# Attention and squared-ReLU MLP on one core: the first chunk's softmax on other engines, and another order of weights and third-chunk work on GpSimd

## The chip, the core and the metric

The kernel runs on one core of a Trainium2 chip. The metric is the device time of one execution in microseconds (us), the median of three runs. The engines are TensorE (PE in the profile: matrix products; PEld: its weight loads), VectorE (DVE), ScalarE (ACT), GpSimd (POOL) and SyncE (SP, which issues the DMAs). SBUF is the on-chip memory, PSUM the banks in which TensorE writes its products.

## The reference

```python
# q, k, v: (8 batches, 8 heads, 576 positions, 64), fp32
scores = q @ k.T / 8
mask_local   = (rel >= 0) & (rel < 32)                    # heads 0 to 3, rel = i - j
mask_strided = (rel >= 0) & (j % 32 == i % 32)            # heads 4 to 7
attn = exp(masked scores - max);  attn /= attn.sum() + 1e-9
x = (attn @ v), heads side by side        # 4608 tokens x 512
h = maximum(x @ w_in, 0)                  # w_in 512 x 2048
out = h * h @ w_out                       # w_out 2048 x 512
```

## The kernel before

The 4608 tokens are cut into 12 chunks of 384. A chunk's attention output x is kept transposed, in a local and a strided half (`xl`, `xs`), each as a high and a low fp32r part (`xlh`, `xll`, `xsh`, `xsl`: the low part is the value less its high part). The MLP of a chunk runs over 16 slices j of 128 hidden units: `up(c, j)` makes 12 products of 128x384 (L462: high by high, low by high, high by low, for four slices of the model dimension), then the squared ReLU and the split into `gh` and `gl` (L470 to L476), and `down(c, j)` adds 9 products of 128x512 to three PSUM accumulators (L489). These 192 steps set TensorE's work.

The weights arrive as raw 64-bit integers and are turned into high and low fp32r parts on the chip during the first chunk, by the generator `convert()`: per half tile a scaling on ScalarE (L154, per whole tile), a conversion into a PSUM bank on ScalarE (`z`, L166), a merge on VectorE that reads that bank (L169), the high cast on ScalarE (L172) and the low subtraction on GpSimd (L173). The weights come in the order w_in 0, w_in 1, w_out 0, w_in 2, w_out 1, and so on; in the rows `w_0`, `w_1` and so on stand for w_in's tiles as for w_out's, numbered apart.

The first chunk's attention has four generators of `pe_pair`, each for two heads: `first` (two local pairs, b_0_1 and b_1_1) and `late` (two strided pairs, b_0_0 and b_1_0). One step of each makes loads, scores and minima (L319, L324), one the exponentials and the normalisation (L345 to L353), one the transposes T and their copies `pt` (L359, L360), one the output products and the split into high and low (L367 and L378, L382 and L383). Local pairs use one exponential per window with its sum taken along (`single`, L345), strided pairs subtract the minimum on GpSimd (L347) and take one exponential per head (L348). The code ahead of the loop calls these steps in an order written out by hand, with runs of zero products (`zeros`, L586) in between, which keep TensorE occupied.

The second chunk has two local pairs of the same kind, and all further chunks `pe_head`. The strided half of later chunks is made by `strided(c)` with elementwise work: products on GpSimd (`pq`, L412), sums on VectorE (L413), a small softmax (L418 to L425), products again (`pp`, L434), sums, transposes, a cast and a subtraction on GpSimd (L446) that writes `xsl`. The blocks 2 and 3 (`pq_2`, `pq_3`) are in the first chunk's time the strided half of the second chunk. `take(c + 2, "010")` starts the heads of the third chunk: their first GpSimd instructions are the subtractions of `kx` and `qx` (L218, L220), which the score products `s` (L234) read.

Each engine runs its instructions in one order. A scheduler sets it when the kernel is built, from the order of the code, the data's dependencies and the marks `issue_after` (an instruction issued no earlier than another); `behind` puts such a mark around one step of a generator. `psum(i, ...)` gives bank i of five. `up` takes the banks 0, 1 and 2 in turn, which hold the first chunk's scores and outputs at the start.

## Time and profile before

| | |
|---|---|
| median of three runs | 884.83 us (883.32 to 884.88) |
| profiled execution | 883.18 us, its span 881.4 us |
| TensorE busy | 868.5 us, 99% of the span |
| VectorE, ScalarE, GpSimd busy | 635.5, 572.6, 676.8 us |

The span goes from the first to the last instruction of the profiled execution; the execution's own time has 1.78 us around it. The shares are averages over a head without dense products (to 30 us), the first chunk with the weights' conversion (to about 114 us), ten chunks that look alike, and the end.

### The profile page before, as it was taken

What the parts mean: (1) busy time and instruction counts of PE and PEld (TensorE: products, weight loads), DVE (VectorE), ACT (ScalarE), POOL (GpSimd) and SP (SyncE); (2) the same over time, 40 slices, a digit from 0 to 9 for tenths busy, and PEclk for the clock granted to TensorE, in tenths of its full rate; (3) what the DMA queues carried; (4) which work ended last, traced back from release to release, by engine and by line L of the source; (5) the groups of instructions that cost most, each with busy time, mean ns of one, the idle gap of its engine ahead of it and who ended that gap; (6) DMA issues with size and microseconds to landing.
All of it is one profiled execution on the core that took longest, in us unless ns stands there. A gap on an engine that the chain in (4) does not pass through costs nothing.

```text
span 881.4 us, 14862 instructions
## 1 busy us (share of the span) xinstructions
PE 868.5 (99%) x4744; PEld 789.6 (90%) x4744; DVE 635.5 (72%) x1892; ACT 572.6 (65%) x1510; POOL 676.8 (77%) x722
## 2 busy tenths in 40 slices
PE   8899999999999999999999999999999999999997
PEld 7788899999999999999999999999999989998996
DVE  4578687788777888878778778778787787883111
ACT  6798776676676666757657747657666665664332
POOL 4698878878978989898988978997898899782000
PEclk9999999999999999999999999999999999999999
DMA  9851631323123123104102302312131121000000
GB/s 356 355 195 63 184 121 42 103 84 113 32 66 112 37 89 103 44 30 127 44 13 80 115 14 74 104 31 74 31 102 57 30 71 61 7 1 10 28 1 36
DMA packets 26798, 71.41 MB, mean 81 GB/s; under 512 B 2976, under 2 KB 8736, under 8 KB 25184
## 3 DMA queue, kind: packets, MB, share of 16 engines
q1 hardware_dynamic: 26432, 70.14, 23.9%
q8 instruction: 37, 0.61, 0.3%
q10 hardware_dynamic: 288, 0.33, 0.1%
q14 instruction: 41, 0.34, 0.1%
HBM read 61.01 MB, written 9.44 MB: 80 GB/s over the span
## 4 chain that ended last, share of the span: by engine, by line
PE 95%; ACT 3%; DVE 1%; POOL 0%; issue 0%; DVEq 0%; POOLq 0%; ACTq 0%
PE h L462 44%; PE y L489 44%; PE s L234 2%; PE o L280 2%; ACT e L345 1%; PE w_ps L586 1%; ACT raw L154 1%; PE b L319 1%; DVE sc L419 0%; ACT z L166 0%; ACT w L172 0%; DVE raw L169 0%; ACT pt L360 0%; PE b L359 0%; DVE xsl L383 0%
## 5 line engine op out<-in xcount | busy, mean ns | idle before, releaser
L489 PE MATMUL y<-w,gh 128*128 128x512 f32 x1152 | 357.1, 391 | 0.8 <-ACT gh L475 0.8
L489 PEld LDWEIGHTS y<-w,gh 128*128 128x128 f32 x1152 | 212.5, 188 | 41.5 <-ACT gh L475 1.4
L462 PE MATMUL h<-xlh,w 128*128 128x384 f32 x768 | 229.6, 339 | 2.1 <-DVE xsl L383 1.6
L462 PE MATMUL h<-xsh,w 128*128 128x384 f32 x768 | 226.2, 335 | 0.0
L489 PE MATMUL y<-w,gl 128*128 128x512 f32 x576 | 224.0, 392 | 0.0
L434 POOL TENSOR_TENSOR pp<-vs,sc 128x448 f32<-128x448 f32 (+10 forms) x192 | 189.8, 1014 | 39.8 <-DVE qs L435 18.2
L412 POOL TENSOR_TENSOR pq<-ks,qs 128x512 f32<-128x512 f32 (+2 forms) x192 | 197.8, 1050 | 17.9 <-DVE sc L413 13.8
L476 DVE TENSOR_TENSOR gl<-h,gh 128x384 fp32r<-128x384 f32 x192 | 105.4, 550 | 84.2 <-ACT gh L475 82.9
L475 ACT CAST gh<-h 128x384 fp32r<-128x384 f32 x192 | 91.4, 477 | 103.0 <-PE y L489 100.0
L473 ACT ACTIVATE h<-h 128x384 f32<-128x384 f32 x176 | 83.0, 472 | 107.8 <-PE h L462 106.2
L413 DVE TENSOR_REDUCE sc<-pq 128x8 f32<-128x512 f32 (+4 forms) x228 | 119.6, 534 | 46.2 <-POOL pq L412 43.9
L462 PEld LDWEIGHTS h<-xlh,w 128*128 128x128 f32 x768 | 142.1, 188 | 5.6 <-DVE xsl L383 1.8
L462 PEld LDWEIGHTS h<-xsh,w 128*128 128x128 f32 x768 | 141.7, 188 | 0.3
L462 PE MATMUL h<-xll,w 128*128 128x384 f32 x384 | 129.3, 337 | 0.0
L435 DVE TENSOR_REDUCE qs<-pp 128x64 f32<-128x448 f32 (+11 forms) x192 | 106.7, 563 | 31.0 <-POOL pp L434 29.5
L489 PEld LDWEIGHTS y<-w,gl 128*128 128x128 f32 x576 | 108.1, 188 | 22.9
L462 PE MATMUL h<-xsl,w 128*128 128x384 f32 x384 | 128.5, 335 | 0.0
L474 ACT ACTIVATE h<-h 128x384 f32<-128x384 f32 x176 | 83.2, 473 | 3.6
L259 DVE STREAM_TRANSPOSE p_t<-e 32x128 f32<-32x128 f32 x240 | 72.3, 301 | 10.4 <-ACT e L248 6.0
L462 PEld LDWEIGHTS h<-xll,w 128*128 128x128 f32 x384 | 72.5, 189 | 2.2
L462 PEld LDWEIGHTS h<-xsl,w 128*128 128x128 f32 x384 | 72.2, 188 | 0.0
L243 ACT ACTIVATE e<-e,nm 96x128 f32<-96x128 f32 x160 | 62.5, 392 | 10.5 <-DVE nm L226 8.8
(97 smaller groups left out, 1077.2 us busy)
## 6 DMA issues: line engine op xcount, KB each, us to landing
qk<-qk_l SPq DMA_DIRECT2D x24, 400.0 KB, 3.2
y<-ysb SPq DMA_DIRECT2D x36, 256.0 KB, 3.7
raw<-w_in SPq DMA_DIRECT2D x7, 1024.0 KB, 11.2
qk<-qk_l SPq DMA_DIRECT2D x16, 416.0 KB, 3.3
vs<-v_s SPq DMA_DIRECT2D x10, 576.0 KB, 4.0
raw<-w_out SPq DMA_DIRECT2D x5, 1024.0 KB, 12.9
v<-v_l SPq DMA_DIRECT2D x40, 128.0 KB, 2.0
ks<-k_s SPq DMA_DIRECT2D x8, 576.0 KB, 3.8
```

Of the source, the lines that this page charges most:

```text
L243: nc.scalar.activation(e[:QC, cut(w)], e[:QC, cut(w)], AF.Exp, bias=nmax[:QC, w : w + 1], scale=-1.0, accum_out=ssum[:QC, w, :1])
L259: nc.vector.transpose(out=pt[STR * k : STR * (k + 1), :, STR * r : STR * (r + 1)], in_=e.rearrange("p (w k) -> p w k", k=KW)[STR * r : STR ...
L412: nc.gpsimd.tensor_mul(pv, kt[:, a : a + m, :], qt[:, i - i0 : i - i0 + 1, :].broadcast_to([P, m, D]))
L413: nc.vector.tensor_reduce(out=sc[:, i - i0, a : a + m], in_=pv, op=ALU.add, axis=AX.X)
L434: nc.gpsimd.tensor_mul(pv, vt[:, a : a + nd, :n], sc[:, il : il + 1, :n].broadcast_to([P, nd, n]))
L435: nc.vector.tensor_reduce(out=ot[:, il, a : a + nd], in_=pv, op=ALU.add, axis=AX.X)
L462: done = nc.tensor.matmul(ph[:, :TC], w[:, wsl], xx, start=n == 0, stop=n == 11)
L473: nc.scalar.activation(g, g, AF.Relu)
L474: nc.scalar.activation(g, g, AF.Square)
L475: last["gh"] = nc.scalar.copy(gh, g)
L476: nc.vector.tensor_sub(gl, g, f32(gh))
L489: done = nc.tensor.matmul(y_ps[c][t], g[:, sl], w[:, wsl], start=j == 0 and k == 0, stop=j == NFT - 1 and k == 2)
```

## The change

In the first chunk the local pairs' exponentials go to PSUM, into the pair's score banks, and VectorE, no longer GpSimd, multiplies them from there by the reciprocal sums into SBUF. The copies of the transposed probabilities of both strided pairs and of local pair 0 (six of eight) move from ScalarE to VectorE. Two runs of 30 zero products become one run of 60 in bank 1 behind the first strided pair's scores. The order of the head's steps is another: the second local pair's exponentials stand behind the first pair's, the second strided pair's scores behind the first pair's multiplies. The split of the first weight is called at once. `up` takes the banks two places on. The weights of a step are no longer asked for behind the strided work of the same step alone: they are gated by `gh` up to step 13 (and by the strided subtraction `xs` in step 13), the heads of the third chunk are started behind them, and the two clears of `p_t` stand behind the last weight on GpSimd. Lines below L177 of before stand 3 to 10 lines further down in the new code (L351 is the old L345, L360 the old L353, L366 and L367 the old L359 and L360, L374 the old L367, L385 the old L378, L419 the old L412, L441 the old L434, L453 the old L446, L469 the old L462); the text names old lines where it doesn't say otherwise.

```diff
--- before.py
+++ after.py
@@ -174,6 +174,9 @@
                     if at and 4 <= k < 12:
                         fetch(k + 4)
 
+                if k == 0 and at:
+                    split()
+                    split = None
                 if not at and k + 1 < NFT and k + 1 in raws:
                     with tc.issue_after(first_step.ins):
                         scale(k + 1)
@@ -313,7 +316,10 @@
         ss = sums[sm]
 
         s_ps = [banks() for _ in range(2)] if c == 0 else None
-        e4 = [e[:QC, : NW * kw].rearrange("p (w k) -> p w k", k=kw) for e in es]
+        blocks = lambda t: t[:QC, : NW * kw].rearrange("p (w k) -> p w k", k=kw)
+        e4 = [blocks(e) for e in es]
+
+        r4 = [blocks(t) for t in s_ps] if single else e4
         def scores(h, w, s):
             rows = slice(D * h, D * (h + 1))
             last["p"] = nc.tensor.matmul(s[:QC, w * kw : (w + 1) * kw], qk[rows, w * QC : (w + 1) * QC], qk[rows, TC + wins[w] : TC + wins[w] + kw], start=True, stop=True)
@@ -342,7 +348,7 @@
         for h in range(2):
             if single:
                 for w in range(NW):
-                    last["a"] = nc.scalar.activation(e4[h][:, w], e4[h][:, w], AF.Exp, bias=nm[:QC, h, w : w + 1], scale=-1.0, accum_out=ss[:QC, NW * h + w, :1])
+                    last["a"] = nc.scalar.activation(r4[h][:, w], e4[h][:, w], AF.Exp, bias=nm[:QC, h, w : w + 1], scale=-1.0, accum_out=ss[:QC, NW * h + w, :1])
             else:
                 nc.gpsimd.tensor_sub(e4[h], e4[h], nm[:QC, h].unsqueeze(2).broadcast_to([QC, NW, kw]))
                 last["a"] = nc.scalar.activation(e4[h], e4[h], AF.Exp, scale=-1.0)
@@ -350,14 +356,15 @@
         nc.vector.tensor_reduce(out=rs[:QC].rearrange("p h w -> p (h w)"), in_=ss[:QC], op=ALU.add, axis=AX.X)
         last["v"] = nc.vector.reciprocal(rs[:QC], rs[:QC])
         for h in range(2):
-            last["g"] = nc.gpsimd.tensor_mul(e4[h], e4[h], rs[:QC, h].unsqueeze(2).broadcast_to([QC, NW, kw]))
+            eng, key = (nc.vector, "v") if single else (nc.gpsimd, "g")
+            last[key] = eng.tensor_mul(e4[h], r4[h], rs[:QC, h].unsqueeze(2).broadcast_to([QC, NW, kw]))
         yield
         p4 = pt.rearrange("p (h w q) -> p h w q", h=2, w=NW)
         for h in range(2):
             t = s_ps[h] if s_ps else banks()
             for w in range(NW):
                 nc.tensor.transpose(t[:kw, w * QC : (w + 1) * QC], e4[h][:, w], ident[:QC, :QC])
-            last["a"] = nc.scalar.copy(pt[:kw, h * TC : (h + 1) * TC], t[:kw, :TC])
+            (nc.vector.tensor_copy if c == 0 and (not local or pr == 0) else nc.scalar.copy)(pt[:kw, h * TC : (h + 1) * TC], t[:kw, :TC])
         yield
         x = x_tiles(c)
         if local:
@@ -443,7 +450,7 @@
             cols = slice(col, col + ni * STR)
             src = xf.rearrange("p a i r -> p a (i r)")
             nc.scalar.copy(x["s", "h"][:, :, cols], src)
-            nc.gpsimd.tensor_sub(x["s", "l"][:, :, cols], src, f32(x["s", "h"][:, :, cols]))
+            last["xs"] = nc.gpsimd.tensor_sub(x["s", "l"][:, :, cols], src, f32(x["s", "h"][:, :, cols]))
             yield 2
 
 
@@ -452,7 +459,7 @@
     def up(c, j):
         x = xt[c]
         p, o = divmod(j, 2)
-        ph = psum((c * NFT + j) % 3, f"h{c}_{j}")
+        ph = psum((c * NFT + j + 2) % 3, f"h{c}_{j}")
         n = 0
         for kt in range(4):
             kind, kk = "ls"[kt // 2], kt % 2
@@ -601,28 +608,30 @@
     next(first[0])
     next(first[1])
     with tc.issue_after(last["p"].ins):
-        zeros(0, NWARM // 2)
         for k in range(NEARLY, 8):
             fetch(k)
     next(late[0])
-    with tc.issue_after(last["p"].ins):
-        zeros(1, NWARM // 2)
+    zeros(1, NWARM)
+    next(first[0])
+    parts = last["v"], last["a"]
+    with tc.issue_after(parts[1].ins):
+        next(first[1])
+    with tc.issue_after(parts[0].ins):
+        next(late[1])
+    next(first[0])
+    weights = behind({"a": last["a"]}, ungated)
+    next(first[1])
+    next(late[0])
+    next(late[1])
+    for _ in range(2):
+        next(weights)
     next(first[0])
     next(first[1])
-    weights = behind({"a": last["a"]}, ungated)
-    next(late[1])
-    for i in range(2):
-        next(first[0])
-        next(first[1])
+    for _ in range(2):
         next(late[0])
         next(late[1])
-        if i:
-            weights = behind({"a": last["a"]}, ungated)
-        for _ in range(2):
-            next(weights)
-    next(late[0])
-    next(late[1])
-    for _ in range(2 * NEARLY - 4):
+    weights = behind({"a": last["a"]}, ungated)
+    for _ in range(2 * NEARLY - 2):
         next(weights)
     heads_end = {e: last[e] for e in "agsv"}
     zbank = (3, 4)
@@ -645,19 +654,20 @@
                             last["mm"] = part(*divmod(i, NFT))
                 last["pe"] = last["mm"]
             take(c + 1, rest)
-        if j == NFT - 2:
-            take(c + 2, "010")
-        if c == 0:
-
-            weights = behind({"a": last["gh"]}, ungated)
+        if s < NFT - 2:
+
+            weights = behind({"a": last["gh"]} | ({"x": last["xs"]} if s > NFT - 4 else {}), ungated)
             for _ in range(WRATE):
-                if next(weights, "end") != "end":
-                    weights_end = {e: last[e] for e in "agsv"}
+                next(weights, "end")
+            weights_end = {e: last[e] for e in "agsv"}
         if s == LATER:
             zbank = (4,)
         if s == NFT - 1:
-            for t in p_t:
-                nc.gpsimd.memset(t, 0.0)
+            with tc.issue_after(weights_end["g"].ins):
+                for t in p_t:
+                    nc.gpsimd.memset(t, 0.0)
+        if j == NFT - 2:
+            take(c + 2, "010")
         if c + 1 < NCHUNK and s >= LATER:
             j0 = LATER if c == 0 else 0
             if j == j0:
```

VectorE in the head, at the first local pair's sums (`rs_0_1`), before; `nm` are a pair's minima:

```order
L324 ISA e_1_1_115,nm_1_1_216<-b_1_1_219,mask_sb 96x128
L324 ISA nm_1_1_216 96x1
L350 TENSOR_REDUCE rs_0_1_197<-sums_94 96x8
L351 RECIPROCAL rs_0_1_197<-rs_0_1_197 96x8
L324 ISA e_0_0_100,nm_0_0_277<-b_0_0_279,mask_sb 96x96
```

and after:

```order
L330 ISA e_0_0_100,nm_0_0_246<-b_0_0_249,mask_sb 96x96
L330 ISA nm_0_0_246 96x1
L356 TENSOR_REDUCE rs_0_1_197<-sums_94 96x8
L357 RECIPROCAL rs_0_1_197<-rs_0_1_197 96x8
L360 TENSOR_TENSOR e_0_1_109<-b_0_1_198,rs_0_1_197 96x512
L360 TENSOR_TENSOR e_0_1_110<-b_0_1_199,rs_0_1_197 96x512
L355 TENSOR_REDUCE sums_96<-e_0_0_100 96x4
L330 ISA w_1_0_104,nm_1_0_351<-b_1_0_354,mask_sb 96x96
```

The first strided pair's eight minima (`e_0_0`), four of which stood right behind the sums, now all stand ahead of them, and behind the sums follow the two multiplies that read the PSUM banks `b_0_1` and were GpSimd's.

TensorE at the first up products (`h_0`), before:

```order
L359 MATMUL b_1_0_355<-ident,w_1_0_104 96x96 x4
L378 MATMUL b_0_0_280<-pt_0_0_103,v_0_0_102 32x96
L378 MATMUL b_1_0_354<-w_1_0_104,v_1_0_106 32x96 x8
L378 MATMUL b_1_0_355<-w_1_0_104,v_1_0_106 32x96 x8
L462 MATMUL h_0_531<-xlh_423,w_0_413 128x384
L462 MATMUL h_0_531<-xll_424,w_0_413 128x384
```

and after:

```order
L366 MATMUL b_1_1_219<-ident,e_1_1_115 128x96 x4
L469 MATMUL h_0_530<-xlh_424,w_0_412 128x384
L469 MATMUL h_0_530<-xll_425,w_0_412 128x384
L374 MATMUL b_1_1_218<-pt_1_1_116,v_1_1_113 64x96
L469 MATMUL h_0_530<-xlh_424,w_0_412 128x384
L385 MATMUL b_0_0_248<-pt_0_0_103,v_0_0_102 32x96 x8
L385 MATMUL b_0_0_249<-pt_0_0_103,v_0_0_102 32x96
L374 MATMUL b_1_1_218<-pt_1_1_116,v_1_1_113 64x96 x7
L385 MATMUL b_0_0_249<-pt_0_0_103,v_0_0_102 32x96 x3
L366 MATMUL b_1_0_353<-ident,w_1_0_104 96x96 x4
L385 MATMUL b_0_0_249<-pt_0_0_103,v_0_0_102 32x96
L366 MATMUL b_1_0_354<-ident,w_1_0_104 96x96 x4
```

The first up products stood behind the last strided output (L378). Now they begin behind the second local pair's transposes, and outputs and transposes of the strided pairs stand between them.

GpSimd at the end of the weights, before (`w_5` and the others are low halves of weights, `pq_3` and `pp_3` the block 3 of `strided`):

```order
L412 TENSOR_TENSOR pq_3_5_0_1049<-qkvs_3_973 128x384
L347 TENSOR_TENSOR e_1_1_688<-e_1_1_688,nm_1_1_953 96x512
L173 TENSOR_TENSOR w_4_937<-raw_744,w_4_937 128x512 x2
L173 TENSOR_TENSOR w_6_1020<-raw_821,w_6_1020 128x512 x2
L353 TENSOR_TENSOR e_1_1_687<-e_1_1_687,rs_1_1_954 96x512
L353 TENSOR_TENSOR e_1_1_688<-e_1_1_688,rs_1_1_954 96x512
L434 TENSOR_TENSOR pp_3_0_0_1061<-qkvs_3_973,sc_3_975 128x64
L434 TENSOR_TENSOR pp_3_1_0_1120<-qkvs_3_973,sc_3_975 128x128
L173 TENSOR_TENSOR w_5_1092<-raw_0_877,w_5_1092 128x512
L173 TENSOR_TENSOR w_5_1092<-raw_512_879,w_5_1092 128x512
L434 TENSOR_TENSOR pp_3_2_0_1123<-qkvs_3_973,sc_3_975 128x192
L434 TENSOR_TENSOR pp_3_3_0_1126<-qkvs_3_973,sc_3_975 128x256
```

and after:

```order
L419 TENSOR_TENSOR pq_3_5_0_1048<-qkvs_3_972 128x384
L173 TENSOR_TENSOR w_7_1159<-raw_0_941,w_7_1159 128x512
L173 TENSOR_TENSOR w_7_1159<-raw_512_943,w_7_1159 128x512
L173 TENSOR_TENSOR w_6_1217<-raw_0_1024,w_6_1217 128x512
L173 TENSOR_TENSOR w_6_1217<-raw_512_1026,w_6_1217 128x512
L441 TENSOR_TENSOR pp_3_0_0_1060<-qkvs_3_972,sc_3_974 128x64
L441 TENSOR_TENSOR pp_3_1_0_1119<-qkvs_3_972,sc_3_974 128x128
L441 TENSOR_TENSOR pp_3_2_0_1122<-qkvs_3_972,sc_3_974 128x192
L441 TENSOR_TENSOR pp_3_3_0_1125<-qkvs_3_972,sc_3_974 128x256
L173 TENSOR_TENSOR w_7_1270<-raw_0_1096,w_7_1270 128x512
L441 TENSOR_TENSOR pp_3_4_0_1128<-qkvs_3_972,sc_3_974 128x320
L441 TENSOR_TENSOR pp_3_5_0_1182<-qkvs_3_972,sc_3_974 128x384
```

The block's last score product stood ahead of ten low halves, six of them between or behind the first output products. Now five low halves stand behind it: four in a row directly, and the first half of the last weight ahead of the last two output products.

## Rows read from the trace of the kernel before

**Rows 1.** The page of the profiled execution, its part 1 (busy time, share of the span and instructions of TensorE) and its part 4 (the chain of work that ended last, shares of the span by engine and line).

```profile
PE 868.5 (99%) x4744; PEld 789.6 (90%) x4744; DVE 635.5 (72%) x1892; ACT 572.6 (65%) x1510; POOL 676.8 (77%) x722
...
PE h L462 44%; PE y L489 44%; PE s L234 2%; PE o L280 2%; ACT e L345 1%; PE w_ps L586 1%; ACT raw L154 1%; PE b L319 1%; DVE sc L419 0%; ACT z L166 0%; ACT w L172 0%; DVE raw L169 0%; ACT pt L360 0%; PE b L359 0%; DVE xsl L383 0%
```

**Rows 2.** Stretches of the first 80 us. Columns: the stretch and its length, then busy time and instructions of TensorE, its weight loads, VectorE, ScalarE and GpSimd, then TensorE's granted clock (1.00 is full speed), the DMA share and GB/s.

```profile
15.00:20.00 5.00, 3.48 (x37) 2.56 (x35) 3.43 (x16) 5.00 (x11) 4.97 (x7) 1.00 1.02 419
20.00:25.00 5.00, 3.05 (x32) 2.08 (x34) 2.58 (x6) 3.49 (x9) 4.09 (x5) 1.00 1.02 416
25.00:30.00 5.00, 3.56 (x67) 2.85 (x66) 1.40 (x3) 4.13 (x8) 1.51 (x2) 1.00 1.01 422
30.00:33.40 3.40, 2.96 (x9) 2.96 (x10) 2.62 (x5) 3.09 (x7) 1.31 (x1) 0.52 1.00 402
40.00:50.00 10.00, 10.00 (x54) 9.31 (x53) 7.48 (x21) 10.00 (x19) 7.24 (x8) 1.00 0.13 50
50.00:60.00 10.00, 10.00 (x53) 8.57 (x51) 8.60 (x24) 9.54 (x18) 10.00 (x11) 1.00 0.56 188
60.00:80.00 20.00, 20.00 (x111) 17.41 (x111) 15.55 (x51) 18.24 (x33) 18.45 (x20) 1.00 0.50 190
```

**Rows 3.** Who TensorE waited for from 30 to 120 us, in total, with the number of waits and the longest.

```profile
PE h L462 <- DVE xsl L383: 1.6, 1, 1.6
PE y L489 <- ACT gh L475: 0.8, 1, 0.8
```

**Rows 4.** TensorE's instructions in order of time, from 30 to 47 us: start, duration, line, tiles, and in brackets the idle time before it and what ended it.

```profile
30.44 0.69 PE L462 MATMUL h<-xlh,w 128*128 128x384 f32 x1 [1.61 <-DVE xsl L383]
...
32.53 0.52 PE L462 MATMUL h<-xsh,w 128*128 128x384 f32 x1
32.85 0.52 PE L462 MATMUL h<-xsl,w 128*128 128x384 f32 x1
...
38.04 0.34 PE L462 MATMUL h<-xsh,w 128*128 128x384 f32 x1
39.17 1.66 PE L489 MATMUL y<-w,gh 128*128 128x512 f32 x6 [0.79 <-ACT gh L475]
```

**Rows 5.** GpSimd's instructions in order of time, from 12 to 30 us: the multiplies of the first chunk's two local pairs.

```profile
12.60 2.03 POOL L353 TENSOR_TENSOR e<-e,rs 96x512 f32<-96x512 f32 x2 [9.74 <-DVE rs L351]
...
16.95 2.03 POOL L353 TENSOR_TENSOR e<-e,rs 96x512 f32<-96x512 f32 x2
```

**Rows 6.** VectorE's instructions in order of time, from 11 to 31 us: the first pair's sums, two of a strided pair's minima, a weight step that reads PSUM, the last strided low halves.

```profile
12.05 0.17 DVE L350 TENSOR_REDUCE rs<-sums 96x8 f32<-96x16 f32 x1 [0.23 <-ACT e L345]
...
17.02 0.24 DVE L324 CUSTOM_DVE_ANT_0 w<-b,mask_sb 96x96 f32<-96x96 f32 x1
...
17.37 0.25 DVE L324 CUSTOM_DVE_ANT_0 w<-b,mask_sb 96x96 f32<-96x96 f32 x1
...
18.65 0.70 DVE L169 SCALAR_TENSOR_TENSOR raw<-raw,z 128x512 uint32<-128x512 uint32 x1
...
29.84 1.61 DVE L383 TENSOR_TENSOR xsl<-b,xsh 64x384 fp32r<-64x384 f32 x3 [1.31 <-ACT xsh L382]
```

**Rows 7.** ScalarE's instructions in order of time, from 34 to 48 us.

```profile
35.98 0.87 ACT L470 ACTIVATE p_t<-h 128x384 f32<-128x384 f32 x2 [0.39 <-PE h L462]
38.63 0.48 ACT L475 CAST gh<-h 128x384 fp32r<-128x384 f32 x1 [1.78 <-DVE h L471]
39.01 0.65 ACT L166 ACTIVATE z<-raw 128x512 uint32<-128x512 uint32 x1
39.58 0.65 ACT L172 CAST w<-raw 128x512 fp32r<-128x512 f32 x1
40.14 1.18 ACT L154 ACTIVATE raw<-raw 128x1024 f32<-128x1024 f32 x1
```

**Rows 8.** GpSimd's instructions in order of time, from 76 to 115 us (x4 and x2: so many in a row).

```profile
79.16 5.15 POOL L173 TENSOR_TENSOR w<-raw,w 128x512 fp32r<-128x512 f32 x4
86.28 2.04 POOL L353 TENSOR_TENSOR e<-e,rs 96x512 f32<-96x512 f32 x2 [1.97 <-DVE sm L422]
...
89.23 2.62 POOL L173 TENSOR_TENSOR w<-raw,w 128x512 fp32r<-128x512 f32 x2
...
95.60 1.83 POOL L434 TENSOR_TENSOR pp<-qkvs,sc 128x320 f32<-128x320 f32 x2
...
102.86 1.02 POOL L446 TENSOR_TENSOR xsl<-qkvs,xsh 128x384 fp32r<-128x384 f32 x1
103.98 1.31 POOL L173 TENSOR_TENSOR w<-raw,w 128x512 fp32r<-128x512 f32 x1
...
106.07 1.16 POOL L218 TENSOR_TENSOR kx<-qk,kx 128x448 fp32r<-128x448 f32 x1
107.31 1.01 POOL L220 TENSOR_TENSOR qx<-qk,qx 64x384 fp32r<-64x384 f32 x1
```

**Rows 9.** The line L419, all its instructions between 40 and 90 us on VectorE: duration least, median and longest, the first and last start, the form.

```profile
L419 DVE TENSOR_TENSOR sc<-sc,mx x2: 189/2040/3891, 42.5 to 80.5; 128x36 f32<-128x36 f32 x2
```

**Rows 10.** TensorE's instructions in order of time, from 105 to 112 us: the start of the second chunk.

```profile
106.21 0.33 PE L462 MATMUL h<-xsh,w 128*128 128x384 f32 x1
106.38 0.33 PE L462 MATMUL h<-xsl,w 128*128 128x384 f32 x1
...
109.62 0.63 PE L234 MATMUL s<-kx,qx 128*96 128x256 f32 x4
```

## The prediction

> **What bounds the kernel now.** I read the page first: TensorE is busy 99% of the span, and the chain of work that ended last is 44% up products and 44% down products [rows 1]. A kernel like that gains only where TensorE is not yet running densely, so next I read the stretches. Before 25 us TensorE is busy for 3.0 to 3.5 of 5 us, from 40 us on it is full, and from 30 to 33.4 us its granted clock is half of full speed [rows 2]. The longest waits of TensorE from 30 us on are 1.6 and 0.8 us, one of each [rows 3]. So what can still be won lies ahead of the first up product (30.44), in the slow clock behind it and in the gap at 38 us. After that the end of the kernel moves one for one with the point at which TensorE last waited.
>
> The reader should see three more things. First, the first up product waits 1.61 us for a VectorE subtraction [rows 4]: its PSUM bank is the one in which the first strided pair's output lies. Second, its products stand 0.32 us apart at 32.5 and 0.17 apart at 106 [rows 4, 10]: that is the lower of the two clock levels (1.2 and 2.4 GHz), and the nine or so products up to 33.4 lose about 1.4 us by it, after a head in which TensorE stood idle again and again. Third, from 40 to 60 us ScalarE is busy 19.5 of 20 us and GpSimd fills the second half (10.00), and 60 to 80 us shows 18.2 and 18.5 of 20 us [rows 2]: the weights' conversion is paced by these two, and TensorE follows close behind.
>
> **The change part by part.** *Head.* GpSimd's four multiplies take 2.03 us per two and wait for VectorE's sums; the first starts at 12.60 [rows 5]. On VectorE a 128x512 operation that reads PSUM takes 0.69 [rows 6], so two cost about 1.3 us: 0.7 us less each time. But the order puts eight minima of the strided pair ahead of the sums. They cost 0.18 each (two in 0.35 by the starts), 1.4 in all; VectorE waited there 0.23 us for the exponentials [rows 6], so about 1.2 us remains as delay and the sums start at 13.2 instead of 12.05. With the 0.4 us of the sums and their reciprocal the first pair's multiply ends at about 14.9 against 14.63: no gain. The second pair's multiply stands behind four more minima, two copies and a weight step on VectorE; I put its end at 20.9 against 18.98 on GpSimd, 2 us later.
>
> The six copies leave ScalarE, which frees 6 x 0.38 = 2.3 us there by the step from the cast of gh, of the same size, to the next start [rows 7], and cost VectorE 6 x 0.54 = 3.2 us at the price of the subtractions of 384 columns [rows 6]. VectorE was busy 3.43, 2.58 and 1.40 of 5 us in the three stretches from 15 us [rows 2], so it has the room in total, but not in order: it becomes the engine on which the head waits. Carried through, the last strided low half is ready at 29.2 to 29.7 if TensorE is at full clock and at about 31.2 at half clock, against 31.45 (the last of three from 29.84 [rows 6]).
>
> *Bank and first up products.* The up products take the bank two places on and the six local products of h_0 stand among the transposes and strided outputs, so the 1.61 us wait goes. What waits then is the strided part of h_0 and h_1, for the same last low half. *Zero products.* Two runs of 30 become one run of 60 that is over at about 15.7. TensorE then has little until about 20 (gaps of 1.6 and 2.3 us by my order of events; it was busy 3.48 of 5 us there before [rows 2]). Before, the clock was full from 15 to 30 us and low from 30 on, in a gap of 1.61 us and after 10.1 busy us of 15 [rows 2, 4], so I expect it to fall earlier now, and to stay low until the up products run. That costs what it costs now, or up to 1.5 us more, since the transposes and outputs run at half speed too.
>
> *ScalarE's queue* turns this into the time of the weights. Up to the fourth cast of gh it has the same work in both kernels, in another order. In before the first squared-ReLU pass starts at 35.98, and a wait of 1.78 us for VectorE follows [rows 7]. In after two z, two casts and one scaling, 2 x 0.57 + 2 x 0.56 + 1.1 = 3.3 us by the steps of the starts and the scaling's length in [rows 7], stand behind that pass and fill such a wait. So ScalarE's lead is 35.98 + 1.78 - 3.2 - T, or 34.6 less T, where T is the start of the first pass in after, and up to 1.3 us less if it waits there for z banks. I put T at 31.2 warm and 33.3 to 34.7 cold. The lead is then 2.0 to 3.4 us warm, and -1.4 to +1.3 cold. **I take a gain of 0.3 us for the head**, near the middle of the cold case with the little slack that TensorE has on the weights.
>
> *Weights ahead of GpSimd's products.* The order now puts six more low halves ahead of the third block's last score product than before (26 against 20), with a subtraction and two multiplies of the second pair, 6 x 1.3 + 1.0 + 2.0 = 10.8 us by [rows 8] (the subtraction as half of the multiplies). That product ended at 78.2 before, a subtraction ahead of 79.16; now it ends at 89, or up to 92 where GpSimd waits for the casts. Four low halves (5.15 us [rows 8]) stand behind it.
>
> At this point the trace has an oddity that matters. VectorE's L419 subtracts two SBUF tiles of 36 elements per lane. It takes 0.19 us at 42.45, and 3.89 us at 80.47, where GpSimd runs four low halves back to back from 79.16 to 84.31 [rows 8, 9]. So a VectorE operation can be held for the whole of such a run. The Trainium skill has a rule for this (SBUF — State Buffer, Who interferes with whom): a VectorE instruction with two SBUF inputs contends with a GpSimd instruction that reads SBUF, and one with at most one SBUF input, outside the two-port modes, does not. By it the new multiplies, which read PSUM and one small SBUF tile, would not be held, and the trace agrees as far as the PSUM subtractions beside GpSimd show no long one. It speaks against the other half of the change: four low halves stand right at L419 again.
>
> From those rows: the softmax of the block can go on at 94 to 97. Its chain of short operations takes some 1.5 us (GpSimd waited 1.97 for it before), the first four output products some 2.0 (they are of 64 to 256 columns, and the two of 320 and 384 take 1.83 [rows 8]). Next stands the first half of the last weight, which started at 103.98 before [rows 8], behind xsl; now the last two products and xsl are behind it. How early it can come hangs on raw buffers: w_out 5's low halves free those for the next weight, and w_in 7's those for the last. The first were at 89.23 before [rows 8] and come 4 to 6 us earlier now, but w_in 7's stand behind the score products and at best gain half of that. I take 101.5. Behind it come the two products, then sums, transposes and the cast of xsh, 1.8 us if VectorE and ScalarE are free (three operations of about 0.6) and 5.4 as in before (97.43 to 102.86). So xsl ends at 101.5 + 1.3 + 1.8 + 1.8 + 1.0 = 107.5 where it ended at 103.88 before: down to 105.4 if the half comes 2 us earlier, and up to 111 with the 5.4. Then come one low half, kx and qx, 1.31 + 1.16 + 1.01 = 3.5 us more [rows 8], so 111.0 (108.32 before).
>
> TensorE needs xsl at 106.38 and qx at 109.62 in before [rows 10]. In after it interleaves h_0 and h_1 of the second chunk: eight more of their products, 0.17 us each [rows 10], and a local pair's outputs stand ahead of the first one with xsl. So it needs xsl at about 108.0, and qx at 109.8. The first is just in time, and **the second costs 1.2 us** (0 to 3.5 over the range). This stall is behind the weights, and nothing later gives it back.
>
> **Sum.** -0.3 + 1.2 = +0.9 us on the profiled execution, 883.18 (span 881.4 and 1.78 around it), which makes 884.1. That execution lies 1.65 under the median of the runs shown (884.83), so the median should be 885.7. Differences under 0.2%, 1.8 us, can't be told from no change by such measurements.
>
> **The rivals.** *Warm start and GpSimd in time (0.27).* If the run of 60 zero products and the earlier local part carry the clock through the head, then h_0 is done near 31, ScalarE leads by 2 to 3.4 us, and TensorE gains about 2.5: 1.4 us of slow clock and the gap of about 1 us at 38 to 39 [rows 4] are what there is to win. With xsl and qx in time the result is 882.3. For it: the 1.61 us wait goes surely, and GpSimd's idle time of 1.97 us in [rows 8] could be used. Against it: TensorE is emptier between 15.7 and 20 than it was.
>
> *GpSimd late at the second chunk (0.22, slower).* The place is the first s product, L234 in before. If L419 is held for the four low halves and the last weight's first half starts as late as before, xsl ends at 109 to 110, between the taken and the upper bound, and qx at 112.5 to 113.5; TensorE stands 2.7 to 3.7 us, and the result is about 888. It decides from qx later than 111.9, where the loss with the head's gain passes 1.8 us. By the skill's rule alone, which makes L419 wait whenever such a run is under way, this would be the likelier outcome; the traced 0.19 shows that it depends on what GpSimd does at that moment.
>
> *VectorE late in the head (0.08, slower).* If the copies and multiplies come 2 us later than I have them, the last low half is ready at 33 and T is 36: ScalarE is 1.4 us behind, and with the 1.2 above the result is 887.4.
>
> *The head's gain is hidden anyway* is part of my forecast: between 0 and 1.3 us of it would only lengthen TensorE's wait for weights.
>
> **How the numbers follow.** Forecast 0.43 (883.1 to 886.6), warm 0.27, GpSimd late 0.22, VectorE late 0.08. Faster 0.27, same 0.43, slower 0.30. The range reaches from the middle of the warm case to beyond the middle of the late case: 882.0 to 889.0; for the forecast alone it is 884.0 to 886.6.
>
> **What the profile of after would show.** Right: VectorE without idle time from 12 to 24 us; TensorE nearly idle from 15.7 to 20 and a granted clock under 1 in some stretch between 20 and 33; no wait at the first up product for xsl, the first squared-ReLU pass between 33 and 35; GpSimd's last score product of the third block near 90; and a wait of about 1 us at the first s product or at the first xsl product near 108 to 110, released by GpSimd. Wrong: a full clock all the way from 15 to 35 with the pass near 31 (the result is then below 883), xsl before 105.5 and no wait after 40 us, or a second L419 that takes 0.2 us beside the low halves.

## The result, and the profile after

The changed kernel is slower: 889.58 us against 883.84 us for the kernel before (medians of 20 runs each on the same chip), a ratio of 1.0057 with a 95% interval of 1.0046 to 1.0068, 5.7 us. The profiled execution took 890.59 us, its span 888.8, so it is 7.4 us over that of before. TensorE's granted clock is 0.988 of full speed in its mean, where the profiled execution of before had 0.997. This mean clock differs between executions of the same kernel, and the time goes with it: of the 20, two had a mean clock of 0.996 and took 883.5 and 883.7 us; four with 0.990 took 888.0 to 889.5, and the rest, with 0.987 to 0.989, 888.7 to 891.2. In the two with the higher clock the change costs nothing.

The stretches of the changed kernel, columns as in [rows 2] (the clock is the third column from the end):

```profile
10.00:15.00 5.00, 4.80 (x74) 4.44 (x72) 4.93 (x40) 4.94 (x25) 1.61 (x2) 1.00 1.01 389
15.00:20.00 5.00, 3.44 (x29) 2.65 (x28) 5.00 (x28) 5.00 (x14) 2.21 (x3) 0.68 1.02 419
20.00:25.00 5.00, 4.73 (x25) 3.74 (x27) 3.56 (x9) 3.40 (x7) 4.08 (x5) 0.50 1.02 423
25.00:30.00 5.00, 5.00 (x44) 3.77 (x42) 1.38 (x3) 0.95 (x2) 1.08 (x2) 0.50 1.01 416
30.00:33.40 3.40, 3.40 (x21) 2.36 (x22) 1.38 (x3) 0.47 (x1) 0.00 (x0) 0.50 0.99 400
33.40:40.00 6.60, 6.60 (x50) 6.14 (x46) 2.50 (x4) 4.28 (x8) 0.88 (x1) 0.71 1.04 399
40.00:50.00 10.00, 7.66 (x36) 5.99 (x36) 7.00 (x15) 10.00 (x19) 6.77 (x9) 1.00 0.14 52
```

The clock falls in the stretch from 15 to 20 us, not at 30, and is at its lower level until the stretch from 33.4 on. From 20.3 to 40 us the profile shows TensorE without idle time. ScalarE, which in the kernel before was busy for 4.13 and 3.09 us of the two stretches from 25 to 33.4, is nearly idle in them (0.95 and 0.47), and VectorE has 1.38 us in each. ScalarE waits for TensorE, as its casts of the strided high halves show (in brackets the idle time before each and what ended it), and VectorE's strided low halves for these casts:

```profile
26.36 0.47 ACT L389 CAST xsh<-b 64x384 fp32r<-64x384 f32 x1 [2.78 <-PE b L385]
...
31.77 0.47 ACT L389 CAST xsh<-b 64x384 fp32r<-64x384 f32 x1 [3.15 <-PE b L385]
...
34.46 0.47 ACT L389 CAST xsh<-b 64x384 fp32r<-64x384 f32 x1 [2.22 <-PE b L385]
```

TensorE's instructions in this time:

```profile
9.97 3.52 PE L593 MATMUL w_ps<-p_t 128*128 128x128 bf16 x60
...
17.26 2.00 PE L374 MATMUL b<-pt,v 128*64 128x96 f32 x16 [0.71 <-DVE pt L367]
20.27 2.79 PE L366 MATMUL b<-ident,e 96*96 96x96 f32 x16 [1.01 <-POOL e L360]
22.77 0.67 PE L469 MATMUL h<-xlh,w 128*128 128x384 f32 x1
...
32.92 2.77 PE L385 MATMUL b<-w,v 96*32 96x96 f32 x32
```

The zero products end at 13.5, then TensorE waits for VectorE and GpSimd. The last 32 strided outputs take 2.77 us at half clock, where before had 1.51 for 30 at full clock:

```profile
27.32 1.51 PE L378 MATMUL b<-w,v 96*32 96x96 f32 x30 [0.28 <-ACT w L360]
```

On VectorE the multiplies from PSUM came about as early as forecast, and the last strided low half, which waits for those outputs, came late:

```profile
13.76 1.28 DVE L360 TENSOR_TENSOR e<-b,rs 96x512 f32<-96x512 f32 x2
...
19.64 1.28 DVE L360 TENSOR_TENSOR e<-b,rs 96x512 f32<-96x512 f32 x2
...
36.24 0.56 DVE L390 TENSOR_TENSOR xsl<-b,xsh 64x384 fp32r<-64x384 f32 x1 [0.72 <-ACT xsh L389]
```

and on ScalarE, where the first squared-ReLU pass answers to the first of [rows 7]:

```profile
39.48 0.87 ACT L477 ACTIVATE p_t<-h 128x384 f32<-128x384 f32 x2 [0.43 <-PE h L469]
```

It starts 3.5 us later than before. GpSimd from 84 to 125 us, to be read against [rows 8]:

```profile
95.07 1.84 POOL L419 TENSOR_TENSOR pq<-qkvs 128x320 f32<-128x320 f32 x2
96.88 5.21 POOL L173 TENSOR_TENSOR w<-raw,w 128x512 fp32r<-128x512 f32 x4
...
112.42 1.00 POOL L453 TENSOR_TENSOR xsl<-qkvs,xsh 128x384 fp32r<-128x384 f32 x1 [2.52 <-ACT xsh L452]
...
115.87 1.00 POOL L223 TENSOR_TENSOR qx<-qk,qx 64x384 fp32r<-64x384 f32 x1
```

and TensorE at the second chunk's start, as in [rows 10]:

```profile
109.75 0.33 PE L469 MATMUL h<-xlh,w 128*128 128x384 f32 x1
...
112.77 0.62 PE L469 MATMUL h<-xlh,w 128*128 128x384 f32 x2 [0.82 <-ACT xlh L389]
...
116.92 0.72 PE L237 MATMUL s<-kx,qx 128*96 128x256 f32 x4 [0.49 <-POOL qx L223]
```

The chunk's first up product in before:

```profile
105.14 0.33 PE L462 MATMUL h<-xlh,w 128*128 128x384 f32 x1
```

It is at 109.75 now; the s product was at 109.62 and is at 116.92. So of 7.3 us, 4.6 come from ahead of the chunk and 2.7 from its start: 1.3 us of waits, 0.8 us of a local pair's outputs that in before stood ahead of the chunk (at 98.69), and the restart of products behind each.

### The profile page after: what moved, and what is told of

It is laid out like the page before. It is cut to its first block, busy times and chain, and to the rows that moved or that the text cites. A ratio compares the mean times of both kernels' runs of the same rounds, so it can differ in the third digit from the quotient of the medians.

```text
span 888.8 us, 14851 instructions
## 1 busy us (share of the span) xinstructions
PE 876.7 (99%) x4744; PEld 794.1 (89%) x4744; DVE 641.6 (72%) x1902; ACT 570.3 (64%) x1504; POOL 672.2 (76%) x718
## 4 chain that ended last, share of the span: by engine, by line
PE 89%; ACT 3%; DVE 3%; POOL 2%; DMA 1%; issue 1%; DVEq 0%; POOLq 0%; ACTq 0%
PE h L469 42%; PE y L496 41%; PE s L237 2%; PE o L283 2%; POOL w L173 1%; DMA raw<-w_out 1%; ACT w L172 1%; ACT raw L154 1%; ACT z L166 1%; PE b L385 1%; PE w_ps L593 1%; DVE e L330 1%; PE b L366 0%; DVE sc L426 0%; POOL pp L441 0%
## 5 line engine op out<-in xcount | busy, mean ns | idle before, releaser
L469 PE MATMUL h<-xlh,w 128*128 128x384 f32 x768 | 231.5, 341 | 2.4 <-ACT w L172 1.2
L441 POOL TENSOR_TENSOR pp<-vs,sc 128x448 f32<-128x448 f32 (+10 forms) x192 | 190.1, 1015 | 48.8 <-DVE qs L442 23.0
L469 PE MATMUL h<-xsh,w 128*128 128x384 f32 x768 | 226.3, 335 | 0.8 <-POOL w L173 0.8
L419 POOL TENSOR_TENSOR pq<-ks,qs 128x512 f32<-128x512 f32 (+2 forms) x192 | 197.7, 1050 | 18.7 <-DVE sc L420 13.2
L469 PEld LDWEIGHTS h<-xlh,w 128*128 128x128 f32 x768 | 142.2, 189 | 7.1 <-ACT w L172 1.6
L469 PEld LDWEIGHTS h<-xsh,w 128*128 128x128 f32 x768 | 141.3, 188 | 1.9 <-POOL w L173 1.1
L469 PE MATMUL h<-xll,w 128*128 128x384 f32 x384 | 129.7, 338 | 0.0
L469 PE MATMUL h<-xsl,w 128*128 128x384 f32 x384 | 128.3, 334 | 0.0
L469 PEld LDWEIGHTS h<-xll,w 128*128 128x128 f32 x384 | 72.8, 190 | 2.6 <-DVE xll L390 0.3
L469 PEld LDWEIGHTS h<-xsl,w 128*128 128x128 f32 x384 | 72.1, 188 | 0.0
```

The source lines that it names most:

```text
L419: nc.gpsimd.tensor_mul(pv, kt[:, a : a + m, :], qt[:, i - i0 : i - i0 + 1, :].broadcast_to([P, m, D]))
L441: nc.gpsimd.tensor_mul(pv, vt[:, a : a + nd, :n], sc[:, il : il + 1, :n].broadcast_to([P, nd, n]))
L469: done = nc.tensor.matmul(ph[:, :TC], w[:, wsl], xx, start=n == 0, stop=n == 11)
```

## The experiments

Two theories stood against each other. *Clock:* TensorE's half speed in the head is the loss. *Order:* the work moved to VectorE, and the weights ahead of GpSimd's products, are the loss, and the clock goes along with it. The filler that most of the runs use writes zero products into 128 columns of a strided pair's score bank which nothing reads. The runs were made in four batches, each with its own runs of before (medians of 883.95 to 884.75 us); the ratio is to those, and times of different batches are compared by it.

| run | median, us | ratio to before, 95% interval | first pass, us |
|---|---|---|---|
| e1, two fillers | 883.88 | 0.9988 (0.9979 to 0.9998) | 32.53 |
| e2, head and bank alone | 891.21 | 1.0085 (1.0068 to 1.0101) | 39.04 |
| e3, loop alone | 884.91 | 1.0006 (0.9998 to 1.0015) | 35.87 |
| e4, bank alone | 883.64 | 0.9998 (0.9985 to 1.0011) | 34.98 |
| e5, zeros apart | 884.76 | 1.0004 (0.9992 to 1.0015) | 36.21 |
| e6, first filler | 882.26 | 0.9984 (0.9972 to 0.9995) | 32.05 |
| e7, fillers, early weights | 877.22 | 0.9925 (0.9911 to 0.9939) | 32.27 |
| e8, fillers, multiplies | 885.57 | 1.0014 (1.0004 to 1.0023) | 33.05 |
| e9, early weights | 881.58 | 0.9975 (0.9966 to 0.9985) | 35.88 |
| e10, first filler, early weights | 879.26 | 0.9946 (0.9933 to 0.9959) | 36.10 |
| e11, before with a filler | 881.73 | 0.9979 (0.9969 to 0.9988) | 35.76 |
| e12, fillers, copies on ScalarE | 883.94 | 0.9994 (0.9984 to 1.0004) | 33.21 |

The last column is the start of the first squared-ReLU pass in the profiled execution (35.98 in before, 39.48 after).

**e1_filled.** The changed kernel, with TensorE occupied in its two gaps:

```diff
     next(first[0])            # transposes of local pair 0
+    fill(1, 14)               # 14 zero products, columns 384:512 of a score bank
     weights = behind({"a": last["a"]}, ungated)
...
     next(first[0])            # outputs of local pair 0
+    fill(1, 26)
     next(first[1])
```

> The changed kernel with 40 more zero products in two gaps of TensorE: 14 behind the second strided pair's scores (its gap at 16.6 us) and 26 behind the first local pair's outputs (its gap at 18.7). They write columns of a score bank that nothing reads; nothing else is edited. Clock theory: the loss is TensorE's half clock from about 17 to 37 us, while its transposes and outputs stand without a gap between 20 and 37 us. With the gaps filled the clock stays full to 30 us at least, the first squared-ReLU pass starts at 31 to 33.5 us instead of 39.5, the mean clock is 0.995 or more, and the time is 881.5 to 884.5 (before is near 884). Rival, the engines' order: VectorE and GpSimd set the head, so the pass stays near 39 us and the time at 888 to 890.

Forty zero products, 2.5 us of work more, take off some 6 us (the ratio goes from 1.0057 to 0.9988). The stretches of this run, and who TensorE waited for up to 140 us:

```profile
15.00:20.00 5.00, 4.93 (x68) 4.23 (x68) 5.00 (x27) 5.00 (x14) 2.34 (x3) 1.00 1.01 416
20.00:25.00 5.00, 4.84 (x66) 3.97 (x67) 4.08 (x10) 3.94 (x9) 3.99 (x5) 1.00 1.01 416
25.00:30.00 5.00, 5.00 (x61) 4.12 (x56) 2.92 (x6) 1.83 (x5) 1.05 (x2) 1.00 1.02 426
```

```profile
PE h L473 <- ACT w L174: 2.0, 2, 1.2
PE h L473 <- POOL w L175: 1.5, 2, 0.8
PE h L473 <- ACT xlh L393: 1.0, 1, 1.0
PE s L239 <- POOL qx L225: 0.5, 1, 0.5
```

TensorE's strided transposes and last strided outputs in this run, which took 2.79 and 2.77 us in the changed kernel:

```profile
20.15 1.65 PE L370 MATMUL b<-ident,e 96*96 96x96 f32 x16
...
27.68 1.51 PE L389 MATMUL b<-w,v 96*32 96x96 f32 x32
```

The clock is full, and the first pass starts 7 us earlier than in the changed kernel. The engines' order is not quite the same: the scheduler also set TensorE's outputs and up products from 22 to 29 us anew, and a few copies and halves on VectorE and ScalarE with them. So this run alone doesn't part the clock from the order. The two executions of the changed kernel at 0.996 do, for they have its order and took 883.5 and 883.7 us. Together they show that the loss needs the low clock.

The order has its share all the same. Of the 95 executions of before in the four batches, 47 had a mean clock of 0.990 or less, and their median is 885.1 us, against 883.6 for the other 48, at 0.993 or more. Such a clock costs before some 1.5 us, and the changed kernel 4 to 8 (888.0 to 891.2 against 883.6). The rows above say why: its head has TensorE without idle time at half clock. That this is the whole difference is not shown, as the other kind of execution of before has no profile.

The run also shows why so little is gained against before: TensorE now waits 3.5 us for weights (ScalarE's casts, GpSimd's low halves) and 1.5 us at the second chunk's start.

**e2_head_only** and **e3_loop_only** take the change apart, each with the other half as in before.

> All of the change ahead of the loop and the bank rotation, with the loop as before (the third chunk's heads ahead of the weights, the clears of p_t unmarked). Clock theory: the loss comes from the head, so 887.5 to 891 with a mean clock of 0.987 to 0.990; the GpSimd order of weights ahead of products comes with the head too. Rival, the loop's new order costs the stall at the second chunk's start (0.8 us for xlh, 0.5 us for qx): 2 to 3 us faster than the changed kernel, 886 to 888.

> The kernel before with only the loop's part of the change (weights ahead of the third chunk's heads and of the clears). Clock theory: the head is untouched, so the clock is that of before and the time differs by what the second chunk's start costs: kx and qx now stand behind the last weight's second half (110.1 to 111.4 us before), so qx comes at about 113.7 instead of 108.3 where TensorE wants it at 109.6, unless the half comes earlier; 0 to 4 us slower, 885 to 887 the likeliest. Rival, the loop part carries the whole loss: 889 to 890.

The head carries the whole loss. The median of e2's six runs is 1.6 us above that of the changed kernel, but the two intervals touch (1.0068 to 1.0101 and 1.0046 to 1.0068), and its profiled execution is 0.5 us shorter, so it is not shown that the loop's part helps this head. In e2 the third chunk's work goes ahead of xsl on GpSimd and TensorE waits 1.5 us for that, in place of the 1.3 us for xlh and qx. By itself the loop's part is within noise; it costs a wait of 0.6 us for qx there. In e2 GpSimd has the weights ahead of block 3's products as in the changed kernel, and in e3 it has not: that order comes with the head, not with the loop.

**e4_bank_only** (`(c * NFT + j) % 3` to `(c * NFT + j + 2) % 3` in the kernel before).

> The kernel before with only the bank of the up products moved two places on. The 1.61 us wait ahead of the first up product goes, and the local products of h_0 run ahead of the last strided low half (31.45 us). The clock falls as in before or not at all, since TensorE has more to do at 28 to 30 us. If TensorE's start is what counts: 0.5 to 2.5 us faster than before (881.5 to 883.5). If the weights' conversion on ScalarE paces this stretch: no change within 0.5 us.

No change: the pass starts 1.0 us earlier, but the clock is as low from 30 to 33.4 us as in before (0.53), and TensorE waits 1.5 us for a strided high half and 2.4 us for gl instead.

**e5_zeros_apart** takes back the merging of the zeros:

```diff
     with tc.issue_after(last["p"].ins):
+        zeros(0, NWARM // 2)
         for k in range(NEARLY, 8):
...
-    zeros(1, NWARM)
+    with tc.issue_after(last["p"].ins):
+        zeros(1, NWARM // 2)
```

> The changed kernel with its 60 zero products put back in two runs of 30, behind the first pairs' and behind the first strided pair's scores, as in before; the steps of the head keep their new order. Theory that the single run of zeros lets the clock fall: the clock stays full to about 30 us as in before and the time is 883 to 885.5. Rival, the clock falls by the head's thinner TensorE work whatever the zeros' places (transposes that wait for VectorE, gaps at 16.6 and 18.7 us): the clock falls before 22 us here too, mean clock 0.987 to 0.991, 887 to 891.

Both hold in part. The time is that of before. But the clock falls here too, at about 20 us, and rises at 30 to 31 (0.90 in the stretch from 30 to 33.4 us), some 6 us sooner than in the changed kernel. The scheduler also set TensorE's order anew, so the place of the zeros is not the only difference.

**e6_fill_first** leaves out the second filler.

> The changed kernel with only the first of the two fillers (14 zero products in the gap at 16.6 us), the gap of 1.5 us at 18.7 left open. If the clock falls by the first gap alone: full clock as with both, 883 to 885. If each gap counts: the clock falls some us later than in the changed kernel, in part of the executions or in all, mean clock 0.988 to 0.996 and 885 to 889.

A gain on both kernels: the clock is full in the profiled execution, and the gap of 1.7 us ahead of the strided transposes does no harm there. TensorE waits for weights as in e1, and for nothing at the second chunk's start, which is where the two differ.

**e7_filled_early** fills ScalarE's idle time of 2.8 us in e1:

```diff
-    for _ in range(2):
+    for i in range(2):
         next(late[0])
         next(late[1])
+        if not i:
+            for _ in range(2):
+                next(weights)
     weights = behind({"a": last["a"]}, ungated)
-    for _ in range(2 * NEARLY - 2):
+    for _ in range(2 * NEARLY - 4):
         next(weights)
```

> Both fillers, and the second weight's two halves asked for between the strided pairs' copies and outputs instead of behind them, so that ScalarE has them to do in its idle time between 23 and 28 us. ScalarE paces the weights from 32 us on, so the lead of up to 2.3 us that the filled kernel has goes on: TensorE's waits for weights (3.5 us in two places by ScalarE and two by GpSimd) shrink by 1.5 to 2.5 us. Theory: 881 to 883 (1 to 2.5 us under the filled kernel's 883.9). Rival, the second chunk's start takes it back (xlh and qx come at GpSimd's pace): 883.5 to 884.5.

The best version, by five runs: 6.6 us under before and some 12 under the changed kernel, well past both expectations. All waits that TensorE has from 7 to 140 us by the same view as in e1:

```profile
PE b L389 <- DVE w L371: 0.7, 1, 0.7
PE y L500 <- ACT gh L486: 0.3, 1, 0.3
PE b L370 <- issue: 0.2, 1, 0.2
```

The 3.5 us for weights and the 1.5 us at the second chunk are gone together: with ScalarE ahead, GpSimd and the second chunk's local pair come in time as well.

**e8_filled_mul** puts the second chunk's multiplies on VectorE (`if single or c == 1`).

> Both fillers, and the multiplies of the second chunk's local pairs on VectorE instead of GpSimd (four of 96x512, both inputs in SBUF). It takes 4 us off GpSimd ahead of the second chunk, and the second pair's outputs come earlier. Theory that GpSimd's queue makes the stall at the second chunk's start (1.0 us for xlh, 0.5 us for qx in the filled kernel): both waits go or halve, 882 to 883.2. Rival, VectorE holds these multiplies while GpSimd runs (as the small subtraction L419 was held 3.9 us) and its squares for the up products come late: no change or slower, 883.5 to 886.

Slower than e1 by some 2 us, as the rival had it. These multiplies have both inputs in SBUF (L364, all four, durations least, median and longest in ns):

```profile
L364 DVE TENSOR_TENSOR e<-e,rs x4: 675/1331/3777, 70.3 to 86.5; 96x512 f32<-96x512 f32 x4
```

The 0.68 us is no exemption: that multiply began at 86.5 together with a low half on GpSimd, and there the low half took 1.85 us instead of 1.30. The four in the changed kernel's first chunk, which read PSUM, while GpSimd was busy beside three of them:

```profile
L360 DVE TENSOR_TENSOR e<-b,rs x4: 676/680/687, 13.8 to 20.2; 96x512 f32<-96x512 f32 x4
```

So the hold is shown; that it makes the 2 us is not. In the profiled execution TensorE waits 3.9 us up to 140 us, less than e1's 5.0 (without the waits of 0.2), and what it lost besides is the clock, which was low from about 35 to 38 us, long before these multiplies. Most of the other executions, with a mean clock of 0.999, took 885.4 to 886.4 all the same; they have no profile.

**e9_early_only** and **e10_first_early**: the early weights with no filler, and with the first.

> The changed kernel with the second weight's halves asked for early, without any filler. Clock theory: the clock falls at about 17 us as in the changed kernel, TensorE needs until 36 to 37 us for the head at half clock, and the first squared-ReLU pass starts at 38.5 to 40; ScalarE does the second weight inside that time, which saves up to 3 us of its work behind the pass, so 885 to 888. Rival, the early weights are what makes the filled and early kernel fast (877.2) and the fillers are not needed: 877 to 880.

> The first filler alone (14 zero products) and the second weight early. With the first filler alone the clock was full in the profiled execution and the time 882.3; with both fillers and the early weights 877.2. Theory: full clock and 876 to 878. Rival, the open gap of 1.5 us at 18.7 lets the clock fall in some of the executions: a wide spread, 877 to 884.

In e9 both sides missed: without a filler, the early weights alone take some 7 us off the changed kernel. The clock falls at 18 us all the same, but rises at 28 instead of 37:

```profile
20.00:25.00 5.00, 5.00 (x34) 4.01 (x34) 3.56 (x9) 4.82 (x9) 4.14 (x4) 0.50 1.01 419
25.00:30.00 5.00, 5.00 (x49) 4.50 (x46) 2.86 (x6) 1.60 (x4) 1.33 (x2) 0.68 1.01 418
30.00:33.40 3.40, 3.40 (x43) 2.72 (x42) 1.43 (x4) 1.81 (x4) 0.00 (x0) 1.00 1.00 404
```

TensorE is busy without a gap in either kernel from 20 us on, with the same instructions in another order, so why the clock rose nine microseconds sooner here stays open. In e10 it is low from 21 to 27 us in the profiled execution, and the runs spread from 877.2 to 880.8: the rival. The second filler brought nothing in e1 (e6 does without it), but with the early weights the five runs that have it are the steadier ones (877.0 to 878.6, in e7).

**e11_before_filled**: the kernel before with 26 zero products behind the second local pair's transposes.

> The kernel before with 26 zero products more, behind the second local pair's transposes (its gap at 19.3 us); nothing else is edited. Theory: the half clock of before from 30.0 to 33.4 us costs 1.4 us and goes when TensorE is occupied more in the head: 882 to 883.5, the clock 1.00 to 40 us. Rival, ScalarE's weights pace what follows, as the ease of the bank alone showed (no change): 883.7 to 884.8.

The median falls by 2.2 us, and the stretch from 30 to 33.4 us reads 1.00, where [rows 2] had 0.52. But in the profiled execution the clock was low earlier instead:

```profile
18.00:20.00 2.00, 2.00 (x18) 1.87 (x15) 1.51 (x5) 2.00 (x4) 1.48 (x3) 0.57 1.02 426
20.00:22.00 2.00, 2.00 (x24) 2.00 (x22) 1.07 (x2) 2.00 (x5) 1.38 (x3) 0.58 1.03 418
```

Its first pass starts only 0.2 us sooner than in before, and the execution is 0.85 us shorter than the profiled one of before. The first up products stand elsewhere too (27.63 against 30.44). So the run shows that before had some 2 us to gain in its head, and not that the half clock behind 30 us cost the 1.4 us that the prediction put on it.

**e12_filled_act**: e1 with its six copies back on ScalarE.

> The changed kernel with both fillers, its six copies of probabilities back on ScalarE; the clock is kept up by the fillers. It measures the copies by themselves. Theory of the prediction (VectorE is what the head waits for, and the copies cost it 3.2 us): with them on ScalarE the last strided low half comes earlier or as early, time 882 to 884, no slower than the filled kernel's 883.9. Rival, ScalarE's queue is what the head waits for, and the six copies free it: 0.5 to 2.5 us slower than the filled kernel, 884.4 to 886.5, the first squared-ReLU pass after 33 us.

The copies' place makes no difference in time, though the pass starts 0.7 us later with them on ScalarE. The clock is full up to the pass in both (in e12's profiled execution it is low from 35 to 39 us, behind it), and at full clock the head has room for the copies on either engine.

## Why the prediction was wrong

The forecast was 885.7 us in a range of 882.0 to 889.0, with 0.30 on slower; 889.58 lies just above that range and nearly 4 us above the forecast.

*The clock.* The forecast had the fall right: in the emptier time behind the zeros, with a low clock until the up products run. It went wrong in the term for it, "what it costs now, or up to 1.5 us more", and in the engine that sets the head's pace. I put the last strided low half at 31.2 us and the pass at 33.3 to 34.7; they came at 36.8 and 39.48. The rows for a better bound were there: [rows 2] show TensorE busy 3.05 + 3.56 = 6.6 of the 10 us from 20 to 30, and at half speed that is up to 13, more than the stretch holds (the same groups of products take 1.7 and 1.8 times as long as in e1). I had VectorE as the engine that the head waits for, and reckoned the slower products as if they still hid behind it; from 20.3 us on it was TensorE. VectorE's own times were right (the pairs' multiplies end at 15.04 and 20.92; I had 14.9 and 20.9), which helped nothing.

*The zeros* ended at 13.5, not 15.7 us, so the emptier time began sooner. The clock fell at about 17 us, and in e5, whose zeros end at 15.0, at about 21. TensorE was not nearly idle then, as I had written, but busy for 3.44 of the 5 us from 15 to 20.

*From the pass to the weights.* The lead "34.6 less T" held. With T = 39.48 it gives -4.9, and the second chunk began 4.6 us later than before; with e1's 32.53 it gives +2.1, and e1's chunk began at 102.81, 2.3 us earlier. e5, e6 and e8, which keep ScalarE's work in the first chunk, come within 0.7 us of it as well. So the step from ScalarE's queue to the second chunk was sound and its input was not. (The sum subtracts 3.2 us where its own rows make 3.3; that changes nothing here.)

*The second chunk's start.* I had 1.2 us for qx. The waits were 1.3 us, but 0.8 of them for `xlh` of the second local pair, whose multiplies the new order also puts behind weights on GpSimd (93.07 after, 86.28 in before), and 0.5 for qx. I had counted that pair's outputs as work and not asked when their copy would be read. GpSimd's last score product came at 96.9, 4.9 us behind my upper bound of 92, about as much as the chunk's start was late.

*L419* (L426 in the new code) was held 3.56 us at its first place, where four low halves now run, and took 0.57 at the second (100.27), beside the four others of 96.88:

```profile
55.61 3.56 DVE L426 TENSOR_TENSOR sc<-sc,mx 128x36 f32<-128x36 f32 x1
...
53.95 5.17 POOL L173 TENSOR_TENSOR w<-raw,w 128x512 fp32r<-128x512 f32 x4
```

The long hold ended with the last of GpSimd's four, at 59.1; the short one at 100.8, when by their mean length the third of them ended. The Trainium skill's rule (SBUF — State Buffer, Who interferes with whom) names two SBUF inputs as the condition, and e8 agrees: 0.68 to 3.78 us for a multiply of two SBUF inputs, 0.68 to 0.69 for the one that reads PSUM. So the rule held in both places: the multiplies were not held in the first chunk, where they read PSUM, and took up to 3.78 us in the second, where both their inputs lie in SBUF.

*The rivals.* "GpSimd late" had the right sign with a wrong place, and "VectorE late in the head" the right place with a wrong engine, and a T of 36 (for 887.4) that was 3.5 us short. "Warm start" is what e1 shows: the clock is full, and of the 3.5 us by which its pass is ahead of that of before, 2.3 are left at the second chunk's first product and none at its s product (110.20 against 109.62), so 883.9 instead of 882.3. The two executions at 0.996 come out at the same time, but have no profile.

*The bank.* The wait of 1.61 us went, as forecast, and by e4 that is worth nothing that can be measured alone.

## What to carry to other kernels

Before moving work ahead of TensorE's dense part, ask what TensorE itself has in the stretch at half clock: up to twice its busy time there, against the stretch's length, says whether it can become the bound. Zero products were cheap here where they stood in the gaps, and one long run ahead of the gaps was not the same as filling them. And an engine that has become idle through a change (ScalarE here) is where to look for the next gain: with the clock kept up, two weight halves asked for earlier brought some 6 us (e7 against e1).

## What the runs showed that I had not expected

The clock stayed low for 20 us, from 17 to 37, and in the last 17 of them the profile shows TensorE busy without a gap (5.00 of 5, 3.40 of 3.40), on transposes and outputs of 96 columns with single up products between them; other orders of the same products had it back after 10 (e5, e9). What brings it back is not shown by these runs. And equal executions of one kernel differ in it: 0.987 to 0.996 in the mean, and 883.5 to 891.2 us with it.
